# Chunk 8's loads moved behind the sixth chunk's output copy on ScalarE's queue, and two pairs of DMA transposes moved ahead of chunk 9's loads

## The chip, the core and the metric

The kernel runs on one core of one Trainium2 chip. The metric is the device time of one execution in microseconds; lower is better. The median of five runs stands for a kernel. One further execution, recorded by the hardware profiler, gives the lines and the times that are quoted here; all positions are microseconds from the start of its span.

## The reference

A linear attention with decay feeds a two-layer feed-forward with SiLU. There are 4 batches, 8 heads, 768 positions and a head size of 64, so 3072 tokens of width 512, and a hidden width of 2048. All inputs and the output are float32.

```
for b in range(nb):                       # blocks of 64 positions
    intra = einsum('bhic,bhjc->bhij', qb, kb) * Dmask      # causal, lam ** (i - j)
    intra = einsum('bhij,bhjd->bhid', intra, vb)
    inter = einsum('bhid,bhde->bhie', qb * lam ** (pos + 1), kv_state)
    out[:, :, sl] = intra + inter
    kv_state = lam ** block * kv_state + einsum('bhsd,bhse->bhde', kb * lam ** (block - 1 - pos), vb)
...
x = out.transpose(0, 2, 1, 3).reshape(3072, 512)
h = x @ w_in
return (h * sigmoid(h)) @ w_out
```

## The kernel before, in words

**Tiling.** The 3072 tokens are cut into 24 chunks of 128 positions (six for each batch), and the chunks into ten groups of two or three (GROUPS). For each chunk the kernel loads q, k and v (load_c, L254: three DMAs of 256 KB, each issued by load_1 at L245), multiplies q and k on GpSimd (POOL) by powers of lam (prep, L367: the products qb at L369 and kb at L363), casts v on ScalarE (ACT) (vcast, L374, at L184), and forms the scores on the tensor engine (PE) (st_s, sp at L491), masks them on VectorE (DVE) (L498), adds the chunk's keys times values to the running state (st_d, L479: PE at L465, copy at L188), and forms the attention output (st_o, L526: op at L522), which ACT copies into the input tile xt of the feed-forward (L530). The feed-forward of a group is the up-projection (ffn1 at L567, or ffn1_two at L553 for groups of two chunks, with its matmuls at L544), SiLU on ACT (g at L549 or L571), and the down-projection (ffn2, L587, matmuls at L593), whose result DVE copies out of PSUM (L597) and SP stores (L585).

**Transposes.** Scores need q and k with the head size on the partitions. Chunks up to 5 are transposed by PE. From chunk 6 on this is done by DMA: dma_t (L382) issues two transposes, qt (L386) and kn (L387), on SP's queue, after POOL's two products. DVE then spreads kn into two zero-padded halves of the buffer ktbd (spread_k, two copies at L188) and the cast values into the halves of vpad (spread_v, four copies at L400). There are four ktbd and four vpad buffers, used in turn, so chunk 8 uses buffer 0 and chunk 9 buffer 1. The first chunks leave other data in them, and clear_halves (L200) has POOL write zeros into buffers 0 and 1 once chunks 4 and 5 are done with them: four memsets (L202, L203).

**What sets the order.** The order of the instructions on each engine is the order of the calls in the program: nothing reorders them. Every engine executes its own instructions in order, and its queue of DMA issues stands in the same order: a DMA that ACT issues comes between ACT's other instructions. Waits between engines are semaphores that the framework places by data and by buffers. DMAs share eight completion semaphores in rotation, so an issue can also wait for the DMA that last used its semaphore.

**The stretch of the change** is L710 to L742, between the attention of the first four chunks and the loop over the groups. It alternates the four down-projections of the first two groups (down0, four steps kk of four output tiles) with the attention of chunks 4 and 5. next_prep (L685) takes the next chunk c: it calls prep(c), then dma_t(c), and then as many load_c of later chunks as its argument says. The loads of chunks 6 and 7 stand above it (L704, L705). After it, the line at L784 starts the up-projections of group 2 (chunks 4 and 5): seven ffn1_two, each of eight matmuls, then an eighth, with the values cast of chunk 6 (vcast) near their beginning, spread_k(6) and spread_v(6) in their middle, and the attention of chunks 6 and 7 from four fifths on. The up-projections write into two PSUM buffers with the tag "h" (L537, and NBUF at L205): the third waits until ACT's SiLU has read the first.

Of the kernel before, what the change touches and what calls it, by code (L numbers as in the profile page):

```python
# [38 lines left out]
def kernel(  # L39
# [10 lines left out]
    nc = tc.nc  # L50
# [149 lines left out]
    def clear_halves(*bufs):  # L200
        for i in bufs:
            nc.gpsimd.memset(ktbd[i], 0.0)  # L202
            nc.gpsimd.memset(vpad[i], 0.0)  # L203
# [38 lines left out]
    def load_1(src, c, tag, bufs, e=None):  # L242
        b, blk = divmod(c, NB)
        t = io.tile([128, H, D], F32, name=tag, tag=tag, bufs=bufs)
        (e or nc.sync).dma_start(out=t, in_=src[b, :, blk * BLK:(blk + 1) * BLK, :].rearrange("h s d -> s h d"))  # L245
        return t

    def load_k(c, e=None):
        rawk[c] = load_1(k, c, "kf", 6, e)

    def load_v(c, e=None):
        vraw[c] = load_1(v, c, "vf", 6, e)

    def load_c(c, e=None):  # L254
        rawq[c] = load_1(q, c, "qf", 4, e)
        load_k(c, e)
        load_v(c, e)
# [109 lines left out]
    def prep(c):  # L367
        qb = nat.tile([128, NP, 2, D], BF16, tag="qb")
        nc.gpsimd.tensor_tensor(qb, rawq.pop(c).rearrange("s (p j) d -> s p j d", j=2), decay(lam_fwd, c % NB),  # L369
                                op=AL.mult)  # L370
        prep_k(c)
        natb[c] = (qb,) + natb[c][1:]

    def vcast(c, e="A"):  # L374
        if c in vraw and c >= NPAD:
            vb = natb[c][2]
            move(e, vb, vraw.pop(c).rearrange("s (p j) d -> s p j d", j=2))
            vnew.add(c)
        elif c in vraw:
            move(e, vpad[c % NKV][:, :, 0:4:3, :], vraw.pop(c).rearrange("s (p j) d -> s p j d", j=2))  # L380

    def dma_t(c):  # L382
        qb, kb, vb = natb[c]
        qt = nat.tile([128, NP, BLK], BF16, tag="qt")
        kn = nat.tile([128, NP, BLK], BF16, tag="kn")
        nc.sync.dma_start_transpose(qt, qb.rearrange("s p j d -> s (p j d)"))  # L386
        nc.sync.dma_start_transpose(kn, kb.rearrange("s p j d -> s (p j d)"))  # L387
        tr[c] = (qt, khalf[c % NKV])
        knat[c] = kn
# [4 lines left out]
    def spread_v(c):  # L394
        if c in vnew:
            vnew.discard(c)
            vb, vh = natb[c][2], vhalf[c % NKV]
            for j in range(2):
                for h in range(2):
                    nc.vector.tensor_copy(vh[64 * j:64 * j + 64, :, h, j, :], vb[64 * h:64 * h + 64, :, j, :])  # L400
# [78 lines left out]
    def st_d(c):  # L479
        vcast(c)  # L480
        pe_d(c)
        copy_kv(c)
# [22 lines left out]
    def pe_o(c, tag="att"):  # L505
        blk = c % NB
        qt, kt = tr.pop(c)
        vb = natb[c][2]
        res = st.pop(c)
        g, off = group_of[c]  # L510
        if off == 0:
            xt[g] = xpool.tile([128, KO_IN, GROUPS[g]], BF16, name="xt", tag="xt", padded_shape=[128, KO_IN, 512])
        op = psum.tile([128, NP, BLK], F32, name="op", tag=tag, bufs=NBUF[tag])
        terms = [(kvb[c][:, p, :], qt[:, p, :], op[:, p, :]) for p in range(NP)] if blk > 0 else []
        for j in range(2):
            if c < NPAD:
                terms += [(vb[:, p, 2 * j:2 * j + 2, :], res[j][:, p, :], op[:, p, :]) for p in range(NP)]
            else:
                terms += [(vhalf[c % NKV][:, p, j, :, :], res[j][:, p, :], op[:, p, 64 * j:]) for p in range(NP)]

        for i, (lhsT, rhs, dst) in enumerate(terms):
            nc.tensor.matmul(dst, lhsT=lhsT, rhs=rhs, start=(i == 0), stop=(i >= len(terms) - NP),  # L522
                             skip_group_check=True)
        return op

    def st_o(c):  # L526
        spread_v(c)
        op = pe_o(c)
        g, off = group_of[c]
        nc.scalar.activation(xt[g][:, :, off * BLK:(off + 1) * BLK], op, AF.Copy)  # L530
# [150 lines left out]
    loads = list(range(8, NCHUNK))  # L681
# [3 lines left out]
    def next_prep(load=1):  # L685
        c = state["prepped"]
        if c < NCHUNK:
            prep(c)
            if c >= NPET:
                dma_t(c)  # L690
            state["prepped"] = c + 1
            for i in range(load):
                if loads:
                    load_c(loads.pop(0))
# [15 lines left out]
    def down0(kk, *mts):  # L710
        for mt in mts:
            ffn2(mt // 2, mt % 2, range(4 * kk, 4 * kk + 4), tag="h" if mt > 1 else "o")
# [14 lines left out]
    down0(2, 0, 1)  # L727
    st_s(5)
    vcast(4), vcast(5)
    load_c(loads.pop(0), nc.scalar)  # L730
    down0(3, 2)
    st_d(4)
    down0(3, 3)
    st_o(4)
    st_d(5)
    next_prep(1)
    next_prep(0)
    next_prep(0)
    down0(3, 0)
    st_o(5)  # L740
    clear_halves(0, 1)
    down0(3, 1)  # L742

# [80 lines left out]
```

## Time and profile before

| what | value |
|---|---|
| median of five runs | 213.6 us (213.25 to 215.66) |
| the profiled execution's own time | 213.33 us |
| its span, from first to last instruction | 211.6 us |
| PE busy (matmuls) | 204.6 us, 97% |
| DVE, ACT, POOL busy | 119.0, 96.4, 53.4 us |
| granted PE clock | 0.998 of full speed |
| moved by DMA | 38.57 MB, 182 GB/s over the span |
| 16 DMA engines, mean busy share 40 to 46 / 46 to 52 / 52 to 58 us | 1.03 / 1.15 / 1.23 |
| three loads of chunk 8, issued by ACT | from 41.80, 42.21, 43.18 us; landing 4.3, 5.5, 6.5 us later |
| three loads of chunk 7, issued by SP | from 42.15, 43.12, 44.16 us; landing 5.7, 5.7, 6.6 us later |
| transposes of chunk 6 (qt, kn) | issued at 46.75 and 48.63 us; landing 4.5 and 3.1 us later |
| three loads of chunk 9, issued by SP | from 49.91, 50.58, 51.16 us; landing 3.5, 3.8, 4.5 us later |
| transposes of chunk 7 | issued at 52.22 and 54.04 us; landing 5.5 and 4.2 us later |
| transposes of chunk 8 | issued at 55.42 and 57.23 us; landing 3.2 and 2.3 us later |
| transposes of chunk 9 | issued at 61.06 and 62.39 us; landing 3.1 and 2.4 us later |

In a line of the list in order of time the columns are: start, time (of a merged run from the first start to the last end), engine, line, operation, tile written and read, shapes, count; in brackets how long the engine was idle before and what ended it. "SPq" and "ACTq" are DMA issues: their time is that of the issuing queue, and the data lands later. In a line of waits, the numbers are the sum in us, how many times, and the longest. A load that lands late, or an engine that is idle, costs nothing as long as PE finds its next operands ready.

### The profile page before, as it was taken

To read this page: it belongs to the slowest core of one execution; us is meant where nothing else is said; L and a number is where in the kernel's file an instruction comes from. 1 tells how busy PE (TensorE), PEld (TensorE's weight loads), DVE (VectorE), ACT (ScalarE), POOL (GpSimd) and SP (SyncE) were. 2 spreads that over 40 slices of the span, in tenths; PEclk is the share of its full clock that TensorE was granted. 3 is DMA by queue.
4 is the path that set the end of the run, shared out by engine and by line. 5 is a ranking of instruction groups with operands and counts; after the bars stand their busy time and mean duration, and the time that the engine had idled before them with its cause. 6 is when DMAs were issued, how large, how long until landed. Compare 5 with 4: busy or idle time off the path is not lost.

```text
span 211.6 us, 4352 instructions
## 1 busy us (share of the span) xinstructions
PE 204.6 (97%) x1698; PEld 127.5 (60%) x1698; DVE 119.0 (56%) x266; ACT 96.4 (46%) x183; POOL 53.4 (25%) x66
## 2 busy tenths in 40 slices
PE   7898999999899999999999999999999999999994
PEld 2466544558656887765665565556565565566654
DVE  3888557695988766664982786457562351110121
ACT  3676672505533764455454544445534344323210
POOL 6360003339803432242333342322000000000000
PEclk9999999999999999999999999999999999999999
DMA  4999999999978999899997999989211011011112
GB/s 112 329 367 404 403 397 253 282 256 245 163 249 197 178 234 214 192 197 163 220 203 185 239 244 159 216 203 202 74 50 54 0 50 54 0 50 50 53 50 99
DMA packets 95573, 38.57 MB, mean 182 GB/s; under 512 B 80960, under 2 KB 88512, under 8 KB 95552
## 3 DMA queue, kind: packets, MB, share of 16 engines
q1 hardware_dynamic: 92288, 37.50, 69.6%
q10 hardware_dynamic: 3264, 0.79, 1.7%
q8 instruction: 13, 0.21, 0.4%
q14 instruction: 8, 0.07, 0.1%
HBM read 27.27 MB, written 6.29 MB: 159 GB/s over the span
## 4 chain that ended last, share of the span: by engine, by line
PE 55%; DMA 25%; SPq 8%; POOL 4%; issue 4%; DVE 2%; ACT 0%; POOLq 0%; DVEq 0%
PE o_ps L593 26%; PE h_ps L567 18%; DMA qf<-in_q_dram 11%; DMA pair<-in_moe_w_out_dram 4%; PE h_ps L544 4%; DMA kn<-kb 4%; DMA kf<-in_moe_w_in_dram 4%; SPq L245 3%; SPq L237 3%; PE op L522 3%; POOL qb L369 2%; DMA pair<-in_q_dram 2%; PE sp L491 2%; PE o_part L608 2%; SPq L387 1%
## 5 line engine op out<-in xcount | busy, mean ns | idle before, releaser
L593 PE MATMUL o_ps<-w_out_bf,g 128*128 128x512 bf16 x368 | 91.7, 379 | 0.0
L593 PEld LDWEIGHTS <-g 128*128 128x128 bf16 x368 | 34.9, 98 | 31.0
L571 ACT ACTIVATE g<-h_ps 128x384 bf16<-128x384 f32 x64 | 31.4, 490 | 46.9 <-PE h_ps L567 46.4
L567 PE MATMUL h_ps<-xt,w_in_bf 128*128 128x384 bf16 x256 | 50.6, 326 | 0.0
L597 DVE COPY ob<-o_ps 128x512 f32<-128x512 f32 x23 | 15.9, 691 | 41.9 <-PE o_ps L593 41.8
L544 PE MATMUL h_ps<-xt,w_in_bf 128*128 128x256 bf16 x288 | 35.8, 273 | 0.5 <-ACT w_in_bf L184 0.5
L369 POOL TENSOR_TENSOR qb<-qf,lam_fwd 128x512 bf16<-128x512 f32 x18 | 18.8, 1044 | 62.8 <-DMA qf<-in_q_dram 53.4
L567 PEld LDWEIGHTS <-w_in_bf 128*128 128x128 bf16 x256 | 23.7, 98 | 17.2
L549 ACT ACTIVATE g<-h_ps 128x512 bf16<-128x512 f32 x36 | 21.3, 597 | 26.1 <-PE h_ps L544 25.9
L544 PEld LDWEIGHTS <-w_in_bf 128*128 128x128 bf16 x288 | 27.2, 98 | 6.1 <-ACT w_in_bf L184 0.7
L498 DVE TENSOR_TENSOR ss<-sp,mask 128x512 bf16<-128x512 f32 (+1 forms) x40 | 21.0, 566 | 14.8 <-PE sp L491 14.4
L188 DVE COPY ktbd<-kn 64x512 bf16<-64x512 bf16 x36 | 18.5, 514 | 7.5 <-DMA kn<-kb 7.1
L400 DVE COPY vpad<-vb 64x256 bf16<-64x256 bf16 x72 | 21.4, 297 | 1.6
L363 POOL TENSOR_TENSOR kb<-kf,lam_bwd 128x512 bf16<-128x512 f32 x20 | 21.1, 1058 | 2.0 <-PE sp L491 1.2
L530 ACT ACTIVATE xt<-op 128x512 bf16<-128x512 f32 x20 | 11.9, 597 | 15.5 <-PE op L522 14.9
L188 DVE CAST kvbd<-kv_ps 64x256 bf16<-64x256 f32 x34 | 14.3, 420 | 8.1 <-PE kv_ps L465 7.7
L491 PEld LDWEIGHTS <-ktbd 128*128 128x128 bf16 x160 | 9.3, 98 | 4.9 <-DVE ktbd L188 1.9
L491 PE MATMUL sp<-qt,ktbd 128*128 128x128 bf16 (+1 forms) x160 | 10.3, 207 | 1.1 <-DVE ktbd L188 1.1
L184 ACT ACTIVATE vb<-vf 128x512 bf16<-128x512 f32 x18 | 11.2, 622 | 0.0
L644 PE MATMUL h_ps<-xt,w_in_bf 128*128 128x512 bf16 x48 | 10.5, 379 | 0.0
L522 PE MATMUL op<-ss,vpad 128*128 128x128 bf16 (+1 forms) x160 | 10.3, 207 | 0.0
L522 PEld LDWEIGHTS <-vpad 128*128 128x128 bf16 x160 | 8.9, 98 | 0.7
(84 smaller groups left out, 131.1 us busy)
## 6 DMA issues: line engine op xcount, KB each, us to landing
out_dram<-ob SPq DMA_DIRECT2D x23, 256.0 KB, 2.6
kf<-in_k_dram SPq DMA_DIRECT2D x19, 256.0 KB, 3.8
vf<-in_v_dram SPq DMA_DIRECT2D x19, 256.0 KB, 4.2
qf<-in_q_dram SPq DMA_DIRECT2D x17, 256.0 KB, 3.3
pair<-in_moe_w_out_dram SPq DMA_DIRECT2D x8, 512.0 KB, 7.7
pair<-in_moe_w_in_dram SPq DMA_DIRECT2D x6, 512.0 KB, 7.6
pair<-in_k_dram SPq DMA_DIRECT2D x4, 256.0 KB, 4.5
pair<-in_q_dram SPq DMA_DIRECT2D x4, 256.0 KB, 4.7
```

Of the source, the lines that this page charges most:

```text
L188: nc.vector.tensor_copy(dst, src)
L363: VG[e].tensor_tensor(kb, rawk.pop(c).rearrange("s (p j) d -> s p j d", j=2), decay(lam_bwd, c % NB), op=AL.mult)
L369: nc.gpsimd.tensor_tensor(qb, rawq.pop(c).rearrange("s (p j) d -> s p j d", j=2), decay(lam_fwd, c % NB), op=AL.mult)
L400: nc.vector.tensor_copy(vh[64 * j:64 * j + 64, :, h, j, :], vb[64 * h:64 * h + 64, :, j, :])
L491: nc.tensor.matmul(sp[:, p, :], lhsT=lhsT, rhs=qt[:, p, a:], start=True, stop=True)
L498: VG[e].tensor_tensor(ss, sp, m[:, None, :n].to_broadcast([128, 4, n]), op=AL.mult)
L522: nc.tensor.matmul(dst, lhsT=lhsT, rhs=rhs, start=(i == 0), stop=(i >= len(terms) - NP), skip_group_check=True)
L544: nc.tensor.matmul(hps[g, i][:, a:a + 256], lhsT=w_in_bf[:, ko, m * 128:(m + 1) * 128], rhs=xt[g][:, ko, :], start=(ko == 0 and u == 0), s ...
L549: nc.scalar.activation(gg.rearrange("p u n -> p (u n)"), hps[g, i], AF.Silu)
L567: nc.tensor.matmul(hp[:, a:z], lhsT=w_in_bf[:, ko, m * 128:(m + 1) * 128], rhs=xt[g][:, ko, a:z], start=(ko == 0 and a == 0), stop=(ko == ...
L571: nc.scalar.activation(gg, hp[:, :n], AF.Silu)
L593: nc.tensor.matmul(o, lhsT=gt[g, ko][:, mt * BLK:(mt + 1) * BLK], rhs=w_out_bf[:, ko, :], start=(ko == 0), stop=(ko == KO_OUT - 1))
```

## The change

Chunk 8's loads, issued through ACT's queue, move from behind the values casts of chunks 4 and 5 to behind st_o(5), whose last instruction on ACT is the copy of chunk 5's output into xt. The first next_prep no longer issues the loads of chunk 9 after the transposes of chunk 6; the transposes of chunk 7 follow those of chunk 6 directly. Chunk 9's loads, on SP, come after st_o(5), and the products and transposes of chunk 8 after them. clear_halves stays behind the products of chunk 8. No instruction is added or taken away.

```diff
     st_s(5)
     vcast(4), vcast(5)
-    load_c(loads.pop(0), nc.scalar)
     down0(3, 2)
     st_d(4)
     down0(3, 3)
     st_o(4)
     st_d(5)
-    next_prep(1)
     next_prep(0)
     next_prep(0)
     down0(3, 0)
     st_o(5)
+    load_c(loads.pop(0), nc.scalar)
+    load_c(loads.pop(0))
+    next_prep(0)
     clear_halves(0, 1)
     down0(3, 1)
```

In the instructions of the two kernels as built, PE, DVE and POOL have the same instructions in the same order. On ACT the three issues of chunk 8's loads stand behind both copies into xt of chunks 4 and 5 in place of ahead of them, and ahead of the values cast of chunk 6. On SP the order becomes: transposes of chunk 6, of chunk 7, one output store, loads of chunk 9, transposes of chunk 8, three output stores, transposes of chunk 9; before it was transposes of chunk 6, loads of chunk 9, transposes of chunks 7 and 8, four output stores, transposes of chunk 9.

## The prediction

> **What bounds the kernel now.** I read the page's busy shares first, then who waited for whom on PE, then the lists of instructions in order of time between 40 and 70 us on PE, ACT, DVE, POOL and SP. From the page:
>
> ```profile
> span 211.6 us, 4352 instructions
> ...
> PE 204.6 (97%) x1698; PEld 127.5 (60%) x1698; DVE 119.0 (56%) x266; ACT 96.4 (46%) x183; POOL 53.4 (25%) x66
> ```
>
> PE is busy for 204.6 of 211.6 us, so a change can gain only what PE idles. All waits of PE, over the whole span:
>
> ```profile
> PE warm_ps L219 <- DVE zero L118: 1.3, 1, 1.3
> PE sp L491 <- DVE ktbd L188: 1.1, 1, 1.1
> PE tk L282 <- POOL kp L266: 0.8, 1, 0.8
> PE h_ps L544 <- ACT w_in_bf L184: 0.5, 1, 0.5
> ```
>
> Only the second lies near the change: the scores of chunk 6 (sp, L491) wait for the copy of its transposed keys into ktbd. Everything else that is loaded late or transposed late in this stretch hides behind PE's other work. In order of time, PE and then DVE and POOL:
>
> ```profile
> 49.47 6.28 PE L544 MATMUL h_ps<-xt,w_in_bf 128*128 128x256 bf16 x56
> 56.80 0.51 PE L491 MATMUL sp<-qt,ktbd 128*128 128x128 bf16 x8 [1.05 <-DVE ktbd L188]
> ```
> ```profile
> 51.80 4.95 DVE L188 COPY ktbd<-kn 64x512 bf16<-64x512 bf16 x2 [1.43 <-DMA kn<-kb]
> 56.78 1.68 DVE L400 COPY vpad<-vb 64x256 bf16<-64x256 bf16 x4
> ```
> ```profile
> 50.95 1.04 POOL L363 TENSOR_TENSOR kb<-kf,lam_bwd 128x512 bf16<-128x512 f32 x1
> 51.93 0.95 POOL L202 MEMSET ktbd<- 128x1024 bf16 x1
> 52.82 0.95 POOL L203 MEMSET vpad<- 128x1024 bf16 x1
> 53.71 0.95 POOL L202 MEMSET ktbd<- 128x1024 bf16 x1
> 54.61 0.95 POOL L203 MEMSET vpad<- 128x1024 bf16 x1
> ```
>
> The two ktbd copies take 4.95 us together; later ones have a median of 292 ns each. The first began at 51.80, when the transposed keys (kn) of chunk 6 landed, and lasted 3.9 us, to 55.71: over the end of POOL's kb and all four memsets of clear_halves. The second lasted 1.03 us, as long as POOL's next product. So a DVE copy from SBUF to SBUF is held by POOL's work, and that makes PE's 1.05 us. Copies out of PSUM are not held (ob at 49.67 took 0.69 us beside busy POOL).
>
> ACT, in the same stretch:
>
> ```profile
> 48.81 0.60 ACT L530 ACTIVATE xt<-op 128x512 bf16<-128x512 f32 x1 [0.94 <-PE op L522]
> 49.30 0.62 ACT L184 ACTIVATE vb<-vf 128x512 bf16<-128x512 f32 x1
> 50.55 0.60 ACT L549 ACTIVATE g<-h_ps 128x512 bf16<-128x512 f32 x1 [0.62 <-PE h_ps L544]
> ```
>
> The 56 matmuls from 49.47 on are seven up-projections (ffn1_two) of eight matmuls, 0.87 us each, into two h buffers. The third starts at 49.47 + 1.74 = 51.21 and needs the first buffer, free when the first g ends, at 51.15. ACT has 0.06 us to spare there.
>
> **The change, part by part.** *Removed:* chunk 8's three loads on ACT's queue at 41.8 us. Nothing was behind them there (ACT idled 4.87 us before the next xt), so ACT gains nothing. The 16 DMA engines, fully busy in 40 to 52 us, lose 768 KB; at the 232 GB/s of 40 to 46 us that is 3.3 us of transfers. Queries of chunk 7 took 5.7 us to land, its values 6.6, and SP's issue of the latter took 2.50 us; all shrink. SP reaches chunk 6's transposes at about 45 us in place of 46.75 (POOL's kb of chunk 6 was done at 45.27), and kn lands at 49.3 to 50.3 in place of 51.7.
>
> *Moved on SP:* transposes of chunk 7 come ahead of chunk 9's three loads (0.57 + 0.53 + 0.97 us of issue), and one output store and those loads now stand ahead of chunk 8's transposes. Chunk 9's loads start near 52 in place of 49.9, chunk 8's transposes near 54 in place of 55.4 (or when POOL's product is ready), and chunk 9's still wait for POOL, near 60 (60.5 to 62.8 by my count, 61.06 to 63.6 before). Chunk 8's keys are copied at DVE 64.77 and chunk 9's at 70.88: four us or more to spare. Cost nothing; if the loads came some 5 us later than I say, PE would wait at chunk 8's scores (67.50).
>
> *Moved on POOL:* its order is unchanged, but the products of chunk 8 now wait for a load issued at 48.85 instead of 41.80. With 3.5 us to land (chunk 9's queries, issued at 49.91) to 4.3 us (those of chunk 8 before), they start at 52.4 to 53.2, and the memsets run from about 54.5 to 58.1, or 55.3 to 58.9, in place of 51.93 to 55.56. POOL is then idle when kn of chunk 6 lands; DVE is free at 50.36, and both ktbd copies are done by about 51, five us ahead of need. **PE's 1.05 us goes.** This is nearly sure: it takes only an idle POOL near 50.5.
>
> *Added on ACT:* the three loads now stand behind the xt of chunk 5, ahead of the values cast vb and the first g. They are issued from 48.85, when ACT has passed that xt. Price: SP's three for chunk 9, at just this time, took 2.22 us from first start to last end (49.91 to 52.13); ACT's own took
>
> ```profile
> 41.80 0.37 ACTq L245 DMA_DIRECT2D qf<-in_q_dram  x1
> 42.21 0.70 ACTq L245 DMA_DIRECT2D kf<-in_k_dram  x1
> 43.18 1.74 ACTq L245 DMA_DIRECT2D vf<-in_v_dram  x1
> ```
>
> 3.12 us, 0.26 of it a wait, with DMA backed up. I take 2.6: the place speaks for the first row, SP's transposes (1.2 to 1.8 us an issue) beside it for the second. The instructions of the changed build also show waits on these loads: the keys' one for the landing of chunk 7's values (about 49), the values' one for kn of chunk 6 (49.3 to 50.3); neither ends later than the issue would start (near 50.1), so 0, up to 1.6 us if kn still lands at 51.7. Behind stand vb (0.49 us to the next start, as from 48.81 to 49.30) and g: the first g starts at 48.85 + 2.6 + 0.49 = 51.94 in place of 50.55, 1.39 late. Less 0.06 to spare, the third up-projection starts **1.33 us late**. With 2.22 it is 0.95, with 3.12 it is 1.85. After that g takes 0.49 us per 0.87 of PE, so ACT catches up and nothing more is lost.
>
> Here a rule speaks about the price. The Trainium skill, "DMA: Bandwidth & Descriptors", section "Issuing engines are not separate DMA queues", says that another issuing engine saves only sequencer time, usually small beside the transfer. Taken so, the loads on ACT cost almost nothing and the change is worth -1.05. The rows differ in what counts: 2.2 to 3.1 us of sequencer time, small beside 4 to 6 us of landing, but ahead of an engine with 0.06 to spare. I use the rows.
>
> *DVE's copies of chunk 6's values* (four into vpad, 222 ns each) follow vb, which ends near 52.1, just as POOL begins chunk 8's products. Some will be held. The skill's "SBUF — State Buffer", section "Who interferes with whom", says that the loser blocks for the other's whole instruction: at most 1.04 us each by that. The row above held one copy through four memsets, 3.9 us, and let it in at the next product. By the rule all four are done by 56 and cost nothing. By the row one caught at the memsets comes free at 58.2, and the masks of chunk 6 behind it start at 58.3; before, they started at 58.48, and their due time is about 58.9 (chunk 6's outputs on PE at 59.98, less 1.02 for both). One caught copy costs 0, two cost 0.3 to 1. I take the row, and 0.1 us.
>
> *Sum* against the profiled execution: -1.05 + 1.33 + 0.1 = **+0.4 us**: span 211.6 to 212.0, that execution's time 213.33 to 213.7. The 1.7 us around the span don't change. The median of the runs, 213.6, is 0.27 above that execution, so I predict 214.0. From 67 us on PE is full, so a shift at 57 us is carried to the end.
>
> **Rivals.** *1, the gain stays.* ACT's loads issue as lightly as SP's or lighter. From -1.05 (loads free) to -0.1 (2.22 us): 212.5 to 213.5. For it: SP's row. Against: the queue would have to be almost free while SP transposes.
>
> *2, slower: the wait that replaces the old one.* The values' load on ACT waits until kn of chunk 6 lands. If SP is no earlier and kn lands at 51.7 as before, that load ends at 51.7 + 0.97 to 1.74, g starts near 53.2 to 53.9, PE loses 2.6 to 3.3 us in place of 1.05: +1.5 to +2.3, so 215.1 to 215.9. A second copy caught by POOL's memsets adds up to 1. It decides from a landing of about 50.1 on, and passes one per cent at about 51.5. Against: 3.3 us of transfers are gone ahead of kn.
>
> *3, the loads come too late.* Chunk 8 or 9 misses its scores at 67.5 or 72.2: +2 to +5, 216 to 219. Needs 5 us beyond my times.
>
> *4, it doesn't do what it says.* The transposes are no earlier and ACT's issue hides in slack: within 0.3 of 213.6. But 0.06 us of slack speaks against it.
>
> **How the numbers follow.** Likeliest, the exchange of one stall for another (0 to +1): 0.58, its own range 213.5 to 214.6. Rival 1: 0.15. Rival 2: 0.19. Rival 3: 0.03. Rival 4: 0.05. The range 213.1 to 216.0 leaves out the better half of rival 1 and the worst of 2 and 3. One per cent (2.1 us, to 211.5 and 215.7) is about what a measurement of this kernel can tell from no change. Faster than that needs more than all the idle time PE has here: 0.02. Slower takes more than half of rival 2 and rival 3: 0.14. Within: 0.84.
>
> **What would show it.** Right: kn of chunk 6 lands by 50.3; both ktbd copies take about 0.6 us, near 50.5; no wait of PE at sp; a new wait of PE at h_ps (L544) for ACT of 0.9 to 1.9 us at about 51.2; three loads on ACT from 48.85; memsets near 55 to 59. Wrong: no PE wait at L544 (rival 1), the values' load on ACT starting after 51 (rival 2), a PE wait at 60 to 73 us on ss, ktbd or vpad (held copies or late loads).

## The result, and the profile after

The changed kernel's median is 213.94 us (212.26 to 216.53, 40 runs), that of the kernel before, measured with it, 215.19 us (212.81 to 217.66, 77 runs; the five runs shown ahead of the prediction had 213.6). The ratio is 0.996, with a 95% interval of 0.9941 to 0.9978: 0.4% faster. Forecast was 214.0 us, but as 0.2% slower; that the two medians of 214 agree is chance, since before itself was 1.6 us slower here than in its first five runs. Beside before on two further chips the ratio was 0.9945 (0.9922 to 0.9968) and 0.9924 (0.9897 to 0.9951).

In the four later batches 66 of 208 runs of the kernel before, but only 1 of 82 of the changed one in all, have a mean granted clock of 0.992 or less, and those of before take 1.6 to 2.1 us longer, so "at full clock" means below that only runs at 0.996 or more are compared, by their means, with two standard errors. At full clock the changed kernel is 1.29 +- 0.49 us faster on one chip (212.86 against 214.15) and 1.30 +- 0.38 us on another (212.84 against 214.14).

The page after, its span and its busy times (the profiled execution took 212.85 us):

```profile
span 211.1 us, 4349 instructions
...
PE 203.8 (97%) x1698; PEld 127.4 (60%) x1698; DVE 113.8 (54%) x266; ACT 96.4 (46%) x183; POOL 53.8 (25%) x66
```

The waits of PE after: the one of 1.05 us on ktbd is gone, and one on ACT's g is new.

```profile
PE h_ps L544 <- ACT g L549: 0.9, 1, 0.9
...
PE sp L491 <- DVE ktbd L188: 0.4, 2, 0.2
```

In order of time, PE, DVE, POOL, then ACT, after:

```profile
48.76 1.91 PE L544 MATMUL h_ps<-xt,w_in_bf 128*128 128x256 bf16 x16
51.58 4.53 PE L544 MATMUL h_ps<-xt,w_in_bf 128*128 128x256 bf16 x40 [0.91 <-ACT g L549]
55.94 0.50 PE L491 MATMUL sp<-qt,ktbd 128*128 128x128 bf16 x8
```
```profile
49.57 0.58 DVE L188 COPY ktbd<-kn 64x512 bf16<-64x512 bf16 x2
51.07 1.80 DVE L400 COPY vpad<-vb 64x256 bf16<-64x256 bf16 x4 [0.93 <-ACT vb L184]
```
```profile
47.14 1.04 POOL L363 TENSOR_TENSOR kb<-kf,lam_bwd 128x512 bf16<-128x512 f32 x1
51.49 1.04 POOL L369 TENSOR_TENSOR qb<-qf,lam_fwd 128x512 bf16<-128x512 f32 x1 [3.31 <-DMA qf<-in_q_dram]
```
```profile
48.10 0.38 ACTq L245 DMA_DIRECT2D qf<-in_q_dram  x1
48.52 0.60 ACTq L245 DMA_DIRECT2D kf<-in_k_dram  x1
49.22 1.14 ACTq L245 DMA_DIRECT2D vf<-in_v_dram  x1
50.41 0.63 ACT L184 ACTIVATE vb<-vf 128x512 bf16<-128x512 f32 x1 [1.72 <-issue]
50.95 1.06 ACT L549 ACTIVATE g<-h_ps 128x512 bf16<-128x512 f32 x2
```

POOL waits for chunk 8's queries from 48.2 to 51.5, just when kn of chunk 6 has landed, so both ktbd copies take 0.58 us in place of 4.95. The three loads fill ACT's queue for 2.26 us, and the third up-projection waits 0.91 us. Every step of the forecast mechanism is there. Between these two profiles the scores of chunk 6 move by 0.86 us, of which 0.71 us was already there at the first up-projection (49.47 against 48.76), and 0.72 us at chunk 4's scores (41.84 against 41.12), ahead of the change. So one pair of profiles shows an exchange of equals; it doesn't show where 1.3 us come from.

### The profile page after: what moved, and what is told of

Its sections match the earlier page's. It is cut to its first block, busy times and chain, and to the rows that moved or that the text cites. A ratio compares the mean times of both kernels' runs of the same rounds, so it can differ in the third digit from the quotient of the medians.

```text
span 211.1 us, 4349 instructions
## 1 busy us (share of the span) xinstructions
PE 203.8 (97%) x1698; PEld 127.4 (60%) x1698; DVE 113.8 (54%) x266; ACT 96.4 (46%) x183; POOL 53.8 (25%) x66
## 4 chain that ended last, share of the span: by engine, by line
PE 55%; DMA 24%; SPq 11%; POOL 4%; DVE 2%; issue 2%; ACTq 1%; ACT 1%; POOLq 0%; DVEq 0%
PE o_ps L593 24%; PE h_ps L567 18%; DMA qf<-in_q_dram 11%; PE h_ps L544 6%; SPq L245 4%; DMA pair<-in_moe_w_out_dram 4%; DMA kf<-in_moe_w_in_dram 4%; DMA kn<-kb 3%; SPq L237 3%; PE op L522 3%; POOL qb L369 2%; DMA pair<-in_q_dram 2%; SPq L387 2%; PE sp L491 2%; PE o_part L608 2%
## 5 line engine op out<-in xcount | busy, mean ns | idle before, releaser
L400 DVE COPY vpad<-vb 64x256 bf16<-64x256 bf16 x72 | 23.7, 330 | 2.5 <-ACT vb L184 0.9
L188 DVE COPY ktbd<-kn 64x512 bf16<-64x512 bf16 x36 | 11.6, 322 | 11.3 <-DMA kn<-kb 10.9
```

Of the source, the lines that this page charges most:

```text
L188: nc.vector.tensor_copy(dst, src)
```

## The experiments

Theories: A, the hold in before costs more than the 1.05 us first seen; B, SP's new order brings the gain; C, between 60 and 100 us SP's queue sets the end; D, its rival: not the queue, but the time that loads and transposes take to land; E, at one clock both kernels are equal. Chip by chip, the means of before at full clock were 213.76, 214.15, 213.95 and 214.14 us in the four batches (e, f, g, h).

**More executions of the two kernels (no edit).**

> The kernel before, one further profiled execution. If the hold is longer in most executions than the 1.05 us first seen: the wait of PE at chunk 6's scores is 1.4 to 2.2 us. If a window of half clock is seen after the first 6 us, it follows a single wait of PE of more than 1.7 us, by at most 3.4 us.

> The kernel before, once more, for the same two readings: a wait of 1.4 to 2.2 us at chunk 6's scores; a window of half clock only behind a wait of more than 1.7 us.

The two executions of before, PE:

```profile
58.91 0.51 PE L491 MATMUL sp<-qt,ktbd 128*128 128x128 bf16 x8 [2.25 <-DVE ktbd L188]
```
```profile
56.88 0.51 PE L491 MATMUL sp<-qt,ktbd 128*128 128x128 bf16 x8 [1.77 <-DVE ktbd L188]
```

The waits are 2.25 and 1.77 us, where 1.4 to 2.2 was expected, and neither execution has a stretch at half clock. Three more kernels have before's code up to there (or its hold with only later DMAs moved). Together:

| execution | PE could start the scores at | they start at | wait |
|---|---|---|---|
| before, first profile | 55.75 | 56.80 | 1.05 |
| before, second | 56.66 | 58.91 | 2.25 |
| before, third | 55.11 | 56.88 | 1.77 |
| SP's order alone | 55.45 | 56.90 | 1.45 |
| before, more PE work at 57 us | 55.08 | 56.79 | 1.71 |
| before, more issues on SP at 61 us | 55.14 | 57.26 | 2.12 |

(The second column is the third less the wait.) The mean wait is 1.72 us. In four of six the scores start at 56.8 to 56.9, whenever PE is ready: the end of the hold is set by POOL's run of memsets, which follows the landing of loads, and PE's lead is thrown away there. In the first profile PE happened to come later than in these others, and so its wait was the shortest. (In f2, below, whose new tile moves other tiles, POOL's memsets run 3.4 us later and the wait is 0.18 us.) POOL in the third execution of before, within 0.1 us of the first profile's times although PE is 0.64 us earlier:

```profile
52.01 0.95 POOL L202 MEMSET ktbd<- 128x1024 bf16 x1
...
54.68 0.95 POOL L203 MEMSET vpad<- 128x1024 bf16 x1
55.60 1.07 POOL L369 TENSOR_TENSOR qb<-qf,lam_fwd 128x512 bf16<-128x512 f32 x1
```

> The changed kernel once more, beside before on one chip. Theory E (at one and the same granted clock the two kernels are equal, and the measured 0.4 per cent comes from how often an execution has a window of half clock, mean 0.992 in place of 1.000: about 1 in 3 of before, 1 in 40 of the changed one): medians at clock 1.000 within 0.2 us of each other, and at most 1 in 10 of the changed kernel's executions at 0.992. Theory A (an exchange that gains in itself): at clock 1.000 the changed one is faster by 0.5 us or more.

> The changed kernel, beside the others on this chip. If the hold costs more in most executions of before than the 1.05 us of the profile first shown: at clock 1.000 it is 0.7 to 1.3 us faster than before, and at most 1 in 10 of its executions are at 0.992. If the two stalls are equal in size, it is within 0.3 us at clock 1.000 and the gain lies in the windows alone.

Measured above: 1.3 us at full clock, 0 of 22 and 0 of 19 runs at 0.992. E falls. That the hold is longer than first seen stands; what it is worth at the end is asked next. The wait on ACT's g was 0.91, 0.84 and 0.72 us in three profiles of the changed kernel. The third also shows that time won is not always kept:

```profile
83.14 0.34 PE L491 MATMUL sp<-qt,ktbd 128*128 128x128 bf16 x3 [1.48 <-DVE ktbd L188]
```

The kept profiles don't locate the 1.3 us. From chunk 4's scores (41 to 43 us, ahead of all that the change moves) to the end of the span, the three executions of before take 169.76, 171.55 and 170.21 us, those of the changed kernel 169.98, 169.27 and 170.72. The means differ by 0.52 us, less than the spread within either kernel.

**The hold alone taken away.**

```diff
-            nc.gpsimd.memset(ktbd[i], 0.0)
-            nc.gpsimd.memset(vpad[i], 0.0)
+            nc.vector.memset(ktbd[i], 0.0)
+            nc.vector.memset(vpad[i], 0.0)
```

> The kernel before, with the four zeroing memsets of buffers 0 and 1 on DVE in place of POOL; nothing else moves. Both theories: the two ktbd copies of chunk 6 take about 0.6 us, since POOL runs no memset beside them, and the 1.05 us wait of PE at sp is gone; no new wait of PE on ACT, since chunk 8's loads stay early. Theory A (the measured gain of the change is an exchange in which the hold by POOL costs more in most executions, about 1.8 us, than in the one profiled): 1.5 to 2.0 us faster than before, ratio 0.991 to 0.993. Theory B (the hold is worth 1.05 us in every execution, and the rest of the gain comes from the new order of SP's queue): 1.0 us faster, ratio 0.995.

Ratio 0.9987 (0.9949 to 1.0026); at full clock 0.21 +- 0.44 us faster. The scores of chunk 6 start at 55.30 without a wait, 1.5 us earlier than in before, and neither theory's gain is there. Its PE waits later:

```profile
82.76 0.51 PE L491 MATMUL sp<-qt,ktbd 128*128 128x128 bf16 x8 [1.69 <-DVE ktbd L188]
```

and 0.48 us more at 100.87. So the hold is not all: what PE wins is taken back at 83 and 100 us. The wait at 83 us is for chunk 11's transposed keys:

```profile
78.21 1.22 SPq L387 DMA_TRANSPOSE kn<-kb  x1
82.11 0.59 DVE L188 COPY ktbd<-kn 64x512 bf16<-64x512 bf16 x2 [2.44 <-DMA kn<-kb]
```

They were issued 0.37 us later than in the first profile of before (77.84), and landed 3.9 us after their issue in place of 3.1; so by these times about 0.8 of the 1.69 us is landing time. All twenty profiles here divide in this way: in the seven where this one transpose took 3.9 to 5.1 us to land, PE waits 0.95 to 3.50 us at chunk 11's scores; in the other thirteen it took 2.4 to 3.2 us, and PE waits 0.63 us at most. One of the seven is the changed kernel's third profile. Why it lands late in some executions is open. The chain that ended last, in the first profile of before, had said so between 66 and 100 us:

```profile
65.98 4.41 DMA qf<-in_q_dram
...
70.55 1.05 POOL qb L369
...
72.03 1.21 SPq L387
...
73.29 3.17 DMA qf<-in_q_dram
...
94.75 4.56 DMA kn<-kb
...
99.63 0.30 DVE ktbd L188
...
99.98 0.51 PE sp L491 x8
```

A load waits for SP to have issued the transposes of an earlier chunk, these for POOL's products, those for the load ahead. PE was full beside it, with 0.09 us of idle time, because it and the chain arrived together. Theory C was formed here; but the chain's longest pieces are landings (4.41, 3.17, 4.56 us), which speak as much for D.

**Is PE or the chain ahead? 0.87 us more for PE, 1.5 us more for SP.** The last up-projection of group 2 executed twice:

```diff
         ffn1_mm(g, i, range(KO_IN))
+        if (g, i) == (2, 7):
+            ffn1_mm(g, i, range(KO_IN))
```

> The kernel before, with the matmuls of group 2's last up-projection executed twice (the result is the same): 0.87 us more for PE at 57 us, behind the wait at chunk 6's scores; nothing else is changed. Theory C (in before, the chain of SP's issues, loads, POOL and transposes sets when the scores at 83 to 100 us can start, and PE arrives there with nothing to lose): most of it is absorbed, 0 to 0.4 us later than before at the same clock. Theory A (PE alone sets the end in both kernels): 0.87 us later.

> The changed kernel, with the same 0.87 us of PE work. The two profiles of the changed kernel show waits of PE of 0 and 0.4 us after 57 us. Theory C: the changed kernel's chain is a little ahead of PE in most executions, so 0.5 to 0.9 us later than the changed kernel alone, and about equal to before with the same addition. Theory A: 0.87 us later than the changed kernel, and still 0.7 to 1.3 us faster than before with the same addition.

Before with it: ratio 0.9994 (0.9970 to 1.0019), at full clock +0.19 +- 0.33 us: most of 0.87 us is absorbed, as C expected. The changed kernel with it: 0.9967 (0.9946 to 0.9989), 0.56 +- 0.33 us under before without it; against the changed kernel alone on other chips about +0.5. But C also expected the two kernels with the addition to be about equal, and at full clock they differ by 0.75 +- 0.34 us, as A expected. So before is not bound by PE alone, and the changed kernel is still ahead of it.

```diff
+    def sp_more():
+        for i in range(3):
+            nc.sync.dma_start(out=lam_sb[:, 2 * i:2 * i + 2], in_=lam_bc_ap[:, 2 * i:2 * i + 2])
...
+            ([(sp_more,)], 0.49, 0.49), ([(next_prep, 2)], 0.5, 0.5))
```

> The kernel before, with three issues of 1 KB more on SP's queue ahead of chunk 9's transposes, written into parts of a tile that has been read long before (no new tile, so no address moves). They took 0.45 to 0.5 us each in the experiment with a new tile. Theory C: all that follows on SP comes about 1.5 us later and the end 1.0 to 1.5 us later than before at the same clock. Theory A: within 0.3 us of before.

> The changed kernel, with the same three issues. Theory C: the chain has 0 to 0.6 us to spare here, so 0.9 to 1.5 us later than the changed kernel alone, with waits on ktbd of 1 us or more near 83 or 100 us. Theory A: within 0.3 us of the changed kernel. The experiment with a new tile lost 6 us and had other times already before its three issues; if that came from the issues and not from the tile's place, this kernel and the one before it lose 5 us or more.

Before with it: ratio 1.0102 (1.0063 to 1.0140), 2.3 us between the medians, for issues that took 1.47 us of SP. The changed kernel with it: 1.0039 (1.0008 to 1.0071) against before, median 216.61, and a wait of 3.50 us on ktbd at 85.23. At full clock the loss is 3.0 +- 0.6 us in before (three runs of six), and in the changed kernel about 1.8 us against it alone on other chips (nine runs of 22). So SP's queue has no room in either kernel, and C is right in sign. It is not right in size, for it expected 0.9 to 1.5 us, and why both lose more than the issues' own time is open: in the profile of the changed kernel the transpose behind the wait of 3.50 us took 5.1 us to land, which C doesn't speak of.

A first form of this test, f2, wrote into a new tile instead:

> The kernel before, with three issues of 4 KB more on SP's queue (lam into a tile that nobody reads), ahead of chunk 9's transposes. Nothing else is changed. Theory C: SP, which has no pause from here to about 100 us, does everything 1.2 to 1.8 us later; the slack of PE near 100 us is 0, so PE waits about that much longer at scores near 83 or 100 us, and the end is 1.0 to 1.8 us later than before at the same clock. Rival: PE sets the end alone, the queue has room: within 0.3 us of before.

It lost 3.2% (1.0325, 1.0264 to 1.0386), 4 us more than the same issues without the tile. Why is open; in its profile from 30 to 60 us queries took a median of 7.2 us to land, in before's 5.7, and that the new tile moves other tiles' addresses wasn't tested by itself.

**The parts of the change.** SP's order alone (before, with chunk 8's loads early):

```diff
-    next_prep(1)
     next_prep(0)
     next_prep(0)
+    load_c(loads.pop(0))
+    next_prep(0)
```

> The kernel before, with only the order on SP changed: transposes of chunks 6 and 7, then the loads of chunk 9, then the transposes of chunk 8; chunk 8's loads stay at their early place on ACT. Theory A: nothing gained, within 0.3 us of before (ratio 0.999 to 1.001), the wait of PE at sp for ktbd stays at about 1 us. Theory B: it brings most of the measured 0.86 us, ratio 0.996 to 0.997.

Ratio 0.9998 (0.9964 to 1.0032), the hold 1.45 us. Alone it brings nothing. The late load alone (the changed kernel with `load_c(loads.pop(1))` between the two `next_prep(0)` in place of the later load of chunk 9), run twice:

> The changed kernel, with chunk 9's loads back at their old place between the transposes of chunks 6 and 7; chunk 8's loads stay behind the copy of chunk 5's output on ACT. Theory A: all of the change's gain is still there, ratio 0.995 to 0.997, the wait of PE at sp gone and one of 0.9 us on ACT's g in its place. Theory B: the gain is gone but for 0.15 us, ratio 0.999 to 1.000.

> The changed kernel with chunk 9's loads at their old place (so that only chunk 8's load has moved), beside the changed kernel on one chip. If the late load is all that counts: within 0.3 us of the changed kernel at clock 1.000 and as few executions at 0.992. If SP's new order counts: slower by 0.5 us or more, with waits of PE on ktbd near 83 us, since chunk 6's keys land at 52 us, and the copies of chunk 6 meet POOL's products of chunk 8.

Ratios 0.9984 (0.9957 to 1.0011) and 0.9972 (0.9943 to 1.0002); at full clock only 0.18 +- 0.37 and 0.21 +- 0.45 us under before, with waits on ACT's g of 0.98 and 1.21 us and, in one profile, 1.78 us on ktbd at 83.41. On the chip of the second, the whole change gains 1.30. So neither part brings the gain by itself. With chunk 9's loads still ahead, SP's load issues meet those of ACT, and chunk 6's keys landed at 52.2 in one of the two; that this is the reason is argued, not shown. Runs at 0.992 are 3 of 44 here. A third pair was not run: the zeros on DVE together with SP's new order, which would tell whether the new order is what lets any gain through.

**Away with the new wait.** Chunk 8's loads on SP, at the same place:

```diff
-    load_c(loads.pop(0), nc.scalar)
+    load_c(loads.pop(0))
```

> The changed kernel, with chunk 8's three loads at the same place but issued by SP. Both theories: PE's new wait of 0.9 us for ACT's first g goes, the hold by POOL at chunk 6 stays away, so 0.9 us faster than the changed kernel: 1.7 us faster than before, ratio 0.992. If the later issues of chunk 9's loads and transposes (some 2 us) reach PE, a wait on ktbd at chunk 9's scores grows from 0.16 us, to 1 us at most.

Ratio 1.0025 (1.0000 to 1.0050): missed. The wait on g is gone, but POOL's run comes 2 us later and now holds the copies of chunk 7 (3.20 us at 58.08): waits of 1.24, 0.46 and 1.06 us on PE at 61.33, 64.48 and 83.45. Two of the three in ACT's gap instead:

```diff
     st_o(4)
+    c8 = loads.pop(0)
+    rawq[c8] = load_1(q, c8, "qf", 4, nc.scalar)
+    load_k(c8, nc.scalar)
...
     st_o(5)
-    load_c(loads.pop(0), nc.scalar)
+    load_v(c8, nc.scalar)
```

> The changed kernel, with two of chunk 8's three loads (q and k) issued by ACT between the output copies of chunks 4 and 5, where ACT idles for 0.94 us; only the load of v stays behind chunk 5's copy. The first g is then about 1 us earlier. PE's wait of 0.8 to 0.9 us on ACT's g near 51 us shrinks to 0.2 us or less; the hold at chunk 6's scores stays away, since kn of chunk 6 lands before POOL has chunk 8's q. If PE sets the end of the changed kernel: 0.5 to 0.8 us faster than it. If SP's chain does: within 0.3 us of it, with new waits of PE on ktbd at 83 or 100 us of as much as was won.

Ratio 0.9947 (0.9907 to 0.9986). Its profile is the best of all, 209.9 us, with no wait on g and 0.20 us on ktbd in all; but its runs spread from 211.26 to 214.39, and its mean of 212.78 equals the changed kernel's 212.84 on that chip (+- 0.65). The 0.7 to 0.9 us that PE no longer waits is not shown to reach the end.

**Loads of chunks 10 and 11 issued by ACT**, to relieve SP (with the zeros on DVE, and in the changed kernel):

```diff
-            ... ([(next_prep, 2)], 0.5, 0.5))
+            ... ([(next_prep, 0)], 0.5, 0.5), ([(act_load,)], 1.03, 1.03), ([(act_load,)], 1.3, 1.3))
```

> The kernel before with the zeroing memsets on DVE (as in the first experiment) and, besides, the loads of chunks 10 and 11 issued by ACT (after group 2's last SiLU, and after chunk 6's output copy) in place of SP. Theory C (between 60 and 100 us the end is set by SP's queue, which issues without a pause: every load, transpose and store of a chunk costs about 5.7 us of it; PE's time won before 66 us is given back at the scores near 83 or 100 us, where the transposed keys come late): SP is 4 us earlier at chunk 10's transposes, PE's waits on ktbd at 83 and 100 us (1.7 and 0.5 us in the first experiment's profile) are gone, span about 210.3 at full clock, 1.3 us under the profiled 211.6 of before, 1.0 to 1.3 us under before's runs at the same clock. Rival D (the waits near 83 and 100 us come from the time that loads take to land, not from the queue): waits of 1 to 2 us remain there, span 211.5 to 212.5.

> The changed kernel, with the loads of chunks 10 and 11 issued by ACT as above. Theory C: PE's waits on ktbd at 71.6 and 99.5 us (0.16 and 0.25 us) are gone, the wait of 0.9 us on ACT's g stays: span about 210.7, 0.4 us under the changed kernel; and more, up to 1 us, in executions where SP was later. Rival D: no change within 0.2 us.

Ratios 1.0185 (1.0127 to 1.0243) and 1.0213 (1.0171 to 1.0255): the design failed, and tells nothing on C against D. In the second, ACT stood at the issue of chunk 11's keys until 67.75, when chunk 9's transposed keys, issued on SP at 62.41, had landed (at 67.7); chunk 7's output copy stood behind it. PE waited 2.90 and 4.22 us for that copy.

**A longer hold.**

```diff
     clear_halves(0, 1)
+    nc.gpsimd.memset(vpad[1], 0.0)
```

> The kernel before, with one zeroing memset more on POOL behind the four (0.9 us; it clears a buffer again). If the hold of DVE's copy by the run of memsets makes PE's wait at chunk 6's scores, that wait grows by 0.9 us, to 2 to 3 us. If a wait of that length brings a window of half clock behind it, at least 8 in 10 executions have mean clocks of 0.992 or less, in place of about 3 in 10. Time: 0.9 us or less for the longer wait and about 1.2 us for the windows, so 1.2 to 2.2 us later than before over all executions. If the windows have another cause: share of 0.992 as in before.

Ratio 1.0018 (0.9993 to 1.0043), at full clock +0.52 +- 0.54 us; 5 of 22 runs at 0.992. PE's wait was 1.61 us, where 2 to 3 was expected. The edit did not lengthen the hold:

```profile
53.04 5.60 DVE L188 COPY ktbd<-kn 64x512 bf16<-64x512 bf16 x2 [1.34 <-DMA kn<-kb]
```

The two copies take 5.58 to 5.60 us in three executions with four memsets, too. The first came free at 57.60, when the fifth memset had just begun (57.52), and the second was held for that memset (0.98 us) in place of POOL's next product (1.07 us). So this run tells nothing on a longer hold, neither of its time nor of the share.

## Why the prediction was wrong

The step that failed is the sum: it set -1.05 us for the hold against +1.33 us for the new wait, and the profiles show -1.72 and +0.82, which turns the sign. A second step failed with it, that a shift at 57 us is carried to the end.

- *"PE's 1.05 us goes. This is nearly sure"*: it went in every profile of the changed kernel. But 1.05 is the term that was mis-sized. Six executions give 1.05 to 2.25, mean 1.72 (the three of before itself 1.69). I took a wait's length, which depends on when PE arrives, for the price of the hold, whose end doesn't move with PE.
- *"the third up-projection starts 1.33 us late"*: 0.72 to 0.91 in three profiles, mean 0.82. Taking 2.6 us for the three issues was wrong; they took 2.26 us, and the lighter row (2.22) was the right one; its own working gave 0.95 us with it. The Trainium skill's rule of "usually small" ("DMA: Bandwidth & Descriptors", "Issuing engines are not separate DMA queues") was not enough either: the rows decide where an engine has 0.06 us to spare.
- *"One caught copy costs 0 ... I take the row, and 0.1 us"*: no wait of PE there; the four vpad copies took 1.80 us and were done at 52.9, ahead of the memsets at 54.24. The 0.1 falls away; in the experiment with chunk 8's loads on SP such a price was real (copies held for 3.20 us, and PE waited 1.24 us for them).
- With the measured terms the sum is -1.72 + 0.82 = -0.90 in place of +0.4. The measured 1.3 us at full clock leaves 0.4, about its error of 0.38 to 0.49. The agreement is not a proof, because by such a sum the hold taken away by itself should have brought 1.72 us, and it brought 0.21 +- 0.44. Nor do the profiles show SP ahead: its last load of queries before 68 us was issued at 65.69 to 65.89 in three of the changed kernel, and at 65.81, 65.98 and 67.41 in three of before.
- *"From 67 us on PE is full, so a shift at 57 us is carried to the end"*: false as a rule. PE and the chain of loads, products and transposes arrive together. Undoing the hold alone brought PE 1.5 us forward at 55 us and was given back at 83 and 100; 0.87 us more PE work cost before 0.19. The term that the forecast put at nothing, SP's new order, is needed: without it the late load gains 0.2 us, with it 1.3. By what way is open.
- *"2, slower: the wait that replaces the old one"*: kn of chunk 6 landed by 49.5, and the issue of the values on ACT, at 49.22, didn't wait. Rival 1, "the gain stays", was right in sign; its mechanism, loads lighter than I took, is 0.5 us of the 1.3 between the two sums; the longer hold is 0.7.
- The forecast of the place, "memsets near 55 to 59", "three loads on ACT from 48.85", held within 1.2 us (54.2 to 58.8 and 48.10 to 48.91 in three profiles).
- *"a change can gain only what PE idles"*: PE's busy time is no constant either. As the profile models it, the same matmuls took 204.5 to 205.1 us in three executions of before, and 203.5 to 204.8 in three of the changed kernel.

Not settled: what makes the transposed keys of chunk 11 land late in some executions; how the late load and the new order gain together what neither gains by itself; and where before's executions at 0.992 lose their clock, for no profile of before fell on one.

## What to carry to other kernels

A wait in one profile is the difference of two arrivals: before pricing it, ask which of the two is pinned, and look at a second execution. A PE at 97% can still be tied with a chain of queue issues; where the chain that ended last runs through a DMA queue for 34 us, time won on PE ahead of it can be given back, as it was at 83 and 100 us here. Ask of each such wait whether the issue or the landing was late: the two look alike in a list of PE's waits. A load issued from a compute engine costs that engine its issue time and whatever semaphore it waits for, so it belongs in that engine's idle gap; there it cost PE no wait, though the time didn't fall measurably.

## What the runs showed of the hardware

One wait of PE of 2.12 us, in before with three issues more on SP, was followed at once by half clock. Busy times by stretch of 3.4 us; columns: length, then PE, PEld, DVE, ACT, POOL busy with counts, PE clock, DMA share, GB/s:

```profile
51.80:55.20 3.40, 3.33 (x31) 2.74 (x28) 3.40 (x1) 2.30 (x5) 3.40 (x5) 1.00 1.16 261
55.20:58.60 3.40, 1.34 (x16) 1.23 (x18) 3.33 (x5) 1.09 (x2) 2.90 (x3) 1.00 0.76 89
58.60:62.00 3.40, 3.25 (x12) 1.49 (x11) 2.51 (x8) 0.60 (x1) 0.00 (x0) 0.50 0.73 254
62.00:65.40 3.40, 3.40 (x30) 1.87 (x29) 2.08 (x7) 1.12 (x2) 0.00 (x0) 1.00 0.29 96
```

PE was busy for 1.34 of 3.40 us, and the next 3.4 us ran at 0.50. The same came with waits of 2.90, 3.50 and 4.22 us; none of the waits up to 1.78 us in these profiles brought it, nor did one of 2.25 and one of 3.11. The Trainium skill ("TensorE: Matmul & The Clock Gate", "What's actually happening") has a window of about 3.4 us that runs free, which would fit if it matters how much of one window a wait fills; no run here tests that. But its advice to keep idle gaps under about 3 us ("Why this matters for your kernels") is too wide here by the second row. Whether before's share of 0.992 comes from its hold in this way is only argued: waits of 2.1 to 2.25 us occur there, those of the changed kernel at that place end at 0.91; but before's wait of 2.25 us left the clock whole, and the run that was to lengthen the hold didn't lengthen it.
